# Last 256 tokens of a gated feed-forward layer by seven products: four more waves in a hand-ordered table

## The chip, the cores and the metric

The kernel runs on one core of a Trainium2 chip. The metric is device time in microseconds (us). The core has five engines that each run their own instructions in order and wait for each other through semaphores: TensorE (PE, matmuls; its weight loads are listed as PEld), VectorE (DVE), ScalarE (ACT), GpSimd (POOL) and SyncE (SP), which only starts transfers (DMAs).

## The reference

Polysketch attention (4 batches, 4 heads, 1088 positions, head width 32) gives x, 4352 tokens by 128. A gated feed-forward layer follows, and the change lies in it:

```
gate = 1.0 / (1.0 + np.exp(-(x @ w_gate)))     # x: 4352 x 128, w_gate: 128 x 1536
val = x @ w_val
return (gate * val @ w_out).astype(np.float32)  # w_out: 1536 x 128
```

All is in float32. The 1536 columns are 12 blocks of 128.

## The kernel before

Tokens are worked in chunks of 512 (TCH); HALF is 256. The ninth chunk (number 8) has 256 tokens. Chunks 0 to 4 go through the layer in waves interleaved with the attention of later batches. Chunks 5 to 7 and the last 256 tokens form the *section* (`section`, L1498), in which every instruction of PE, ACT, DVE and POOL is issued in the order of a table, `ORDER` (L19), written out by hand; each engine takes its own items in that order. SP's transfers are issued where the items that call for them stand.

For chunks 5 to 7 gate and value come from Winograd's form of Strassen's scheme: a 2x2 block product by seven products instead of eight. The 2x2 blocks are the two halves of the 128 model features (64 rows of the array each) by two turns of tokens. `load_y` (L443) copies x so that both halves of the features lie in rows 0 to 63 and in rows 64 to 127; `x_sum` (L453, items T) forms four differences of tokens on POOL; `cross_weights` (L463) has made three sums of the weights (fw). One wave covers a pair of the 12 blocks; there are 6 waves for a chunk, 18 in all (w = 0 to 17).

Items of the table, each with a number behind the colon:

- **P1 to P7** (`feature`, L1539): one of the seven products for one block of the wave (the accent marks the second block). An item is two matmuls of 64 rows x 64 columns with 256 tokens. For even waves P1, P2, P3, P5 use the array's low 64 rows (LO) and P4, P6, P7 the high ones (HI); for odd waves the other way round. Two matmuls fill the two column halves of one side, so a LO item and a HI item together fill all four quadrants.
- **Aa, Ac, Sa, Sc** on ACT and **D1, D2, M1, M2** on DVE (`gated`, L1585): Aa copies P1's result to the third bank so that P6, P7, P4 go on from there; Ac copies P5's; D1 and D2 add on DVE; Sa, Sc are sigmoids; M1, M2 multiply gate and value into g. A wave's order is P1, P5; Aa, Ac; P2, P6; D1; P3, P7; D2; P4; Sa, Sc; M1, M2. It uses three PSUM banks, A, C and V, two sets of them in turn (`GA`, `GC`, `V`, L1511).
- **Q0 to Q3** (`token_sum`, L1607): four differences of g on POOL, each 128 x 256. Q0 needs M2, Q1 needs M1 and M2, Q2 needs Q1, Q3 needs Q2.
- **W..** (`w_out`, L1561): the output product, again by seven. WL uses the low rows, WU the high rows (two matmuls of 64 x 64), WF all 128 (two of 128 x 64). The third letter is the bank (A, B), the number the pair of blocks and a part. WxB:p.0 needs Q1 and Q3 of p, WxA:p.0 needs M1 and Q2, WxA:p.1 needs M2 and Q0. Pairs -2 and -1 are the last two of chunk 4, whose sums were formed before the section.
- **EA, EB** (`empty`, L1620) copy the output banks on ACT and start transfers that swap halves (on SP, for chunk 7 on ACT itself: one or two each for EA, three for EB); **F0 to F6** (`total`, L1639) add these up on DVE, transpose, and start four stores on SP.
- For the last 256 tokens (`last`, L1656) the table has plain products: **C0 to C3** are gate and value of a pair of blocks (an item is two matmuls of 128 x 64 with 256 tokens), **Y** the sigmoid, **Z** the product, which also reorders the tokens, and **O0 to O3** the output product (two matmuls of 128 x 64 with 128 columns). `store_end` (L552) copies two banks and stores them from ACT's and SP's queues.

Of the kernel before, what the change touches and what calls it, by code (L numbers as in the profile page):

```python
# [19 lines left out]
WUB:-2.0 P1:0 T0:1 P1':0 P5:1 P1':1 P5:0 P1:1 WLA:-2.1 Aa:0 P5':0 P5':1 Aa:1 P2':0 P6':0 P6:0 P2:0  # L20
Ac:0 P2':1 P6':1 Ac:1 D1:0 P2:1 P6:1 Sa:0 D1:1 P3:0 P7':0 P3':0 P7:0 T2:1 P7':1 P3:1 Sc:0 D2:0 P7:1
P3':1 Sa:1 P1:2 WUB:-1.0 D2:1 P5:2 P4':0 Sc:1 P1':2 P4:0 P4:1 P1:3 M1:0 P1':3 P4':1 P5:3 P5':2 Aa:2
M1:1 WUB:-1.1 WLA:-1.0 Ac:2 P6':2 WLA:-2.0 M2:1 P2:2 P6:2 Aa:3 P2':2 P5':3 Q0:1 D1:2 P6':3 P2':3
Ac:3 P6:3 P2:3 M2:0 Q1:1 P7':2 P3':2 Sa:3 P7:2 WLA:-1.1 D1:3 Q0:0 Sa:2 P3:2 P1:5 D2:2 P7:3 P3:3 Q2:1
Sc:2 P3':3 P7':3 P5:4 P4:2 T1:1 Sc:3 D2:3 P4':2 P1:4 Q3:1 P1':4 WUA:-2.0 M1:2 P5:5 P5':4 Q1:0 P1':5
P4':3 M2:2 Aa:4 WUA:-2.1 P4:3 Ac:4 Q2:0 P2:4 P6':4 M1:3 WLB:-2.0 P6:4 Q3:0 P2':4 WUA:-1.0 Aa:5 D1:4
WLB:-1.1 WUA:-1.1 P6:5 P5':5 M2:3 EA:-1 P7:4 P6':5 Sa:4 P3:4 P7':4 Q0:3 P3':4 P2:5 Ac:5 D2:4
WLB:-1.0 WUA:1.0 Q0:2 Sc:4 P1:6 P2':5 D1:5 P4':4 P1':6 EB:-1 T3:1 P4:4 P7':5 Sa:5 P3':5 P7:5 Q1:2
M1:4 WUA:1.1 P5':6 Q1:3 P1':7 P5:6 D2:5 Aa:6 P3:5 WLB:1.1 Ac:6 M2:4 P6':6 P2:6 Q2:3 P4:5 P6:6 Sc:5
P4':5 WUA:0.1 Q0:4 D1:6 WUA:0.0 WLB:1.0 Q3:3 P1:7 WLB:0.0 M1:5 P7:6 P3':6 M2:5 Q2:2 Aa:7 P7':6 P3:6  # L30
P2':6 P5:7 Sc:6 Q1:4 D2:6 P6:7 P5':7 P2':7 P6':7 F0:-1 Ac:7 T0:2 WLA:3.0 P2:7 WLA:0.0 P4':6 D1:7
Q3:2 Sa:7 P5':8 P4:6 M2:6 Sa:6 P5:8 WUB:1.1 Q2:4 P3':7 P7':7 M1:6 P3:7 P7:7 Q3:4 P1':8 P1':9 Sc:7
D2:7 P1:9 P1:8 Q0:5 Ac:8 WLA:0.1 WUB:0.0 P5:9 P4':7 Aa:8 M2:7 Q0:6 P4:7 WUB:3.0 WLA:3.1 WUB:1.0 Q1:5
M1:7 WLA:1.0 P6':8 WLA:2.1 P6:8 F1:-1 T2:2 Aa:9 P5':9 WLA:2.0 D1:8 WUB:2.0 WLA:1.1 Ac:9 WUB:3.1 P6:9
Q0:7 P7:8 P6':9 P7':8 P3:8 D1:9 Q1:7 P3':8 P2:9 P2':8 P2':9 D2:8 Q2:5 Sc:8 P3:9 P2:8 P3':9 P7:9 M2:8
Q1:6 Sa:8 P4':8 P7':9 Sc:9 P4:8 WLB:3.0 Q3:5 D2:9 WUA:2.0 WLB:2.0 Sa:9 WUA:2.1 WLB:3.1 M1:8 WUA:4.0
P4:9 Q0:8 M2:9 P4':9 P1:11 WUA:4.1 P1:10 Q1:8 M1:9 P1':10 P1':11 P5:11 P5':10 F2:-1 Q2:7 Aa:10 P5:10
WUA:3.0 F3:-1 Aa:11 WUA:3.1 WLB:5.0 Q3:7 F4:-1 P6:10 P2:10 Ac:10 P6':10 WLB:5.1 Q2:6 P6:11 P5':11
D1:10 WUA:5.0 WLB:4.0 Q0:9 Ac:11 WUA:5.1 P6':11 F5:-1 P7':10 P3':10 T1:2 D1:11 P7:10 P3:10 P2':11
P2':10 Q1:9 Sc:10 D2:10 P2:11 P7:11 Sa:10 P7':11 P3:11 T3:2 M2:10 P4:10 WLA:5.1 Sa:11 Q3:6 P4':10  # L40
WLA:5.0 D2:11 P3':11 WLA:4.0 Q2:8 WLA:4.1 WUB:4.0 M1:10 Sc:11 P4':11 WUB:5.1 EA:0 P4:11 WUB:5.0
M2:11 P1':13 P1:12 EB:0 P1:13 P1':12 M1:11 Q0:11 P5:13 P5:12 Aa:12 P5':13 P5':12 F6:-1 Q0:10 Aa:13
WUB:7.0 WLA:7.0 P6:12 WLA:6.0 Ac:12 Q1:10 P6':12 P6':13 Ac:13 WUB:7.1 P2:12 D1:12 Q2:10 P6:13
WUB:6.0 P2':13 WLA:7.1 F0:0 Q1:11 P7':12 P3:12 D1:13 P7:12 P3':12 Q3:10 WLA:6.1 P2:13 Sc:12 D2:12
P3':13 P2':12 Q2:11 P3:13 P7':13 M2:12 Sa:12 P7:13 P4:12 Q3:11 Sc:13 WLB:6.0 P4':12 D2:13 P1:14
WUA:6.0 Sa:13 Q3:8 WLB:7.1 WUA:6.1 M1:12 P4:13 P5':15 Q2:9 M2:13 P4':13 P1:15 WUA:7.0 P1':14 Q3:9
M1:13 WUA:7.1 WLB:7.0 Aa:14 P5:14 P1':15 Q0:12 F1:0 P5:15 P5':14 Aa:15 F2:0 P6:14 P2':14 Q0:13 Ac:14
P6':14 WLB:10.0 WLB:11.0 WUA:9.1 Q1:12 Ac:15 D1:14 WUA:8.1 P6':15 WUA:10.1 P6:15 F3:0 Q2:12 P7':14
P3':14 D1:15 P7:14 P3:14 P2:14 WUA:9.0 Sc:14 D2:14 WUA:10.0 WLB:11.1 Sa:14 WLB:9.1 WUA:11.0 M2:14
WLB:8.0 P4':14 WLB:9.0 P4:14 F4:0 P7:15 WUA:11.1 M1:14 P7':15 P3:15 WUA:8.0 P1':16 D2:15 P1:16  # L50
P3':15 P5':16 P2':15 F5:0 Sc:15 P5:16 P2:15 Aa:16 P4':15 WUB:9.1 P5':17 WLA:8.1 Sa:15 WUB:8.0
WLA:8.0 Ac:16 WLA:10.1 P6:16 M2:15 Q0:14 P6':16 P4:15 WLA:9.1 WUB:9.0 Q1:13 D1:16 P1':17 P2:16
WLA:9.0 P1:17 M1:15 Q3:12 P3:16 P7':16 Aa:17 P3':16 P7:16 Q0:15 WLA:10.0 P5:17 Sc:16 D2:16 WUB:10.0
WLA:11.1 Q2:13 Ac:17 WLA:11.0 P2':17 M2:16 P6':17 P2:17 Q3:13 EA:1 P4:16 P6:17 WUB:11.0 P2':16 Q1:15
D1:17 P4':16 WLA:12.0 Sa:16 Q1:14 WUB:11.1 WLA:13.0 Sa:17 P3':17 P7:17 M1:16 Q0:16 P7':17 P3:17 C1:1
Sc:17 D2:17 Q1:16 C0:1 C3:1 M2:17 Y:1 Q2:16 C2:1 EB:1 C0:0 Z:1 Q0:17 P4:17 WUA:13.0 WLB:13.1
WUA:12.0 Q2:14 F6:0 WLB:12.0 WUA:12.1 WLB:13.0 WUA:13.1 Q3:16 F0:1 C1:0 Q3:14 C2:0 F1:1 Y:0 C3:0
F2:1 Q2:15 C0:3 Z:0 C1:2 Q3:15 WUB:13.1 P4':17 WLA:13.1 WUB:12.0 M1:17 WUB:13.0 WLA:12.1 F3:1 C1:3
# [9 lines left out]
def kernel(  # L68
# [367 lines left out]
    def halves(w):  # L436
        return (HI, LO) if w % 2 else (LO, HI)
# [5 lines left out]
    def load_y(c):  # L443
        t = sbA.tile([P, 2 * H * W1], F32, tag="qp", name="yt")
        y = t[:, : 2 * TCH].rearrange("p (k t) -> p k t", k=2)
        s = t[:, 2 * TCH : 4 * TCH].rearrange("p (u t) -> p u t", u=4)
        YT[c] = y, s
        t0 = tok_chk[SECT + c][0]
        for k, src in enumerate((LO, HI)):
            for dst in (LO, HI):  # L450
                nc.sync.dma_start(out=y[dst, k], in_=xT[src, t0 : t0 + TCH])

    def x_sum(c, u):  # L453
        y, s = YT[c]
# [97 lines left out]
    def store_end(acc):  # L552
# [4 lines left out]
        for u, eng in enumerate((nc.scalar, nc.sync)):  # L557
            eng.dma_start(
                out=bass.AP(
                    tensor=out.tensor,  # L560
                    offset=out.offset + (b * S + r // 32 + u) * DM,
                    ap=[[T * DM, 32], [2 * DM, 4], [1, DM]],
                ),
                in_=o_sb[u],
            )
# [932 lines left out]
    def section():  # L1498
# [22 lines left out]
        sgs = [x[:, : 2 * TCH // 32].rearrange("p (j t) s -> p j (t s)", j=2) for x in sgs]  # L1521
# [11 lines left out]
        def g_of(p):  # L1533
            return held[p][0] if p < 0 else gs[p % len(gs)]
# [4 lines left out]
        def feature(k, nn, w):  # L1539
            lead, tail = halves(w)  # L1540
            j = 2 * (w % per) + nn
            f, gate, val = fw[0][:, :, j], w_sb[:, 0, j], w_sb[:, 1, j]
            y, s = YT[w // per]
            even = w % 2 == 0
            rows, lhsT, rhs, dst = {
                "P1": (lead, gate if even else f[:, 0], y[:, 0, :HALF], GA),
                "P2": (lead, f[:, 0] if even else gate, y[:, 1, :HALF], GA),
                "P5": (lead, f[:, 1], s[:, 0], GC),
                "P3": (lead, f[:, 2], y[:, 1, HALF:], GC),
                "P6": (tail, f[:, 1], s[:, 1], V),  # L1550
                "P7": (tail, f[:, 2 if even else 0], s[:, 2], V),
                "P4": (tail, val if even else f[:, 2], s[:, 3], V),
            }[k]
            start = k in ("P1", "P5") and (k, w) not in started
            for c in range(2):
# [200 lines left out]
```

## Time and profile before

| what | us |
|---|---|
| median of three runs | 283.95 (283.89 to 284.19) |
| span of the profiled execution | 282.5 |
| median less span (what lies around the span) | 1.45 |
| PE busy | 276.7 |
| start of the section's first matmul, from the timeline | 177.27 |
| end of the last matmul | 278.99 |
| the 24 C items (96 records) of PE, busy | 11.5 |
| Y (6 of ACT), busy; Z (6 of DVE), busy | 3.6; 6.7 |
| POOL in the section (72 Q, 8 T, 4 sums of the last held pair) | 65.7 of 101.75 |

The profile's page gives busy time of each engine, 40 slices of the span, the chain of work that ended last, and groups of instructions by line. "L530 PE MATMUL b<-yt,fw 64*64 64x256 f32" is a matmul of line 530 that reads tile yt and weights fw, on 64 rows and 64 columns of the array, with 256 columns streamed. Every float32 matmul leaves two such records. A record lasts longer than the spacing to the next one on its quadrant, since its end includes the drain; spacing is read from start to start. The timeline lists start, length, engine, line, operation and count, and in brackets how long the engine had idled and for whom.

### The profile page before, as it was taken

The page shows a single profiled execution, that of the slowest core. Times are in us where ns is not written, and L with a number is a line of the kernel's source. Part 1 is how long each engine was busy: PE and PEld are TensorE (multiplying, and loading weights), DVE is VectorE, ACT ScalarE, POOL GpSimd, SP SyncE. Part 2 cuts the span into 40 slices and gives each one's busy share as a digit, 9 for nine tenths or more (in the row PEclk, how much of TensorE's full clock was granted, in tenths as well). Part 3 has the DMA queues.
Part 4 walks back from the last instruction along what each step waited for, and adds up shares of the span by engine and source line. Part 5 has one row for each costly group of instructions (what it writes and reads, how often), then busy time and mean ns, then how long its engine had stood idle before and what let it go on. Part 6 is the DMA issues. An engine that isn't in the chain of part 4 may idle for free.

```text
span 282.5 us, 7859 instructions
## 1 busy us (share of the span) xinstructions
PE 276.7 (98%) x3204; PEld 158.6 (56%) x3204; DVE 208.3 (74%) x339; ACT 119.6 (42%) x232; POOL 179.7 (64%) x234
## 2 busy tenths in 40 slices
PE   8899999999999999999999999999999999999994
PEld 3554433354444444544444444577788888875674
DVE  6986789847687777786768857577788968579462
ACT  3689742322326222443225223666554554452130
POOL 2666674567575668664778765547798988197300
PEclk9999999999999999999999999999999999999999
DMA  7995540674681267376348520200310031003133
GB/s 210 334 372 144 119 157 15 167 155 138 198 182 43 41 179 151 95 151 182 74 130 155 134 45 15 64 0 18 89 25 2 2 71 19 2 21 66 24 64 57
DMA packets 33332, 29.02 MB, mean 103 GB/s; under 512 B 19216, under 2 KB 27728, under 8 KB 33296
## 3 DMA queue, kind: packets, MB, share of 16 engines
q1 hardware_dynamic: 28880, 25.44, 37.0%
q10 hardware_dynamic: 4416, 3.08, 4.2%
q8 instruction: 25, 0.41, 0.6%
q14 instruction: 11, 0.09, 0.1%
HBM read 20.60 MB, written 3.26 MB: 84 GB/s over the span
## 4 chain that ended last, share of the span: by engine, by line
PE 97%; ACT 1%; POOL 0%; DVE 0%; issue 0%
PE wave L682 37%; PE b L530 24%; PE prod L530 23%; PE moeout L574 4%; PE warm L379 2%; PE kvz L1027 1%; PE nps L1385 1%; PE kps L808 1%; PE moeout L530 1%; PE kvz L1014 1%; PE cqps L954 1%; PE nps L1217 0%; PE denj L1156 0%; PE nps L1169 0%; PE dps L1198 0%; ACT asb L925 0%
## 5 line engine op out<-in xcount | busy, mean ns | idle before, releaser
L682 PE MATMUL wave<-xT,w_sb 128*64 128x512 f32 (+2 forms) x436 | 117.5, 589 | 0.1
L530 PE MATMUL prod<-tsum,ws 64*64 64x256 f32 (+1 forms) x348 | 81.1, 379 | 0.0
L690 ACT ACTIVATE sg<-wave 128x512 f32<-128x512 f32 x60 | 35.8, 597 | 89.3 <-PE wave L682 85.2
L520 POOL TENSOR_TENSOR tsum<-g,tsum 128x256 f32<-128x256 f32 x48 | 47.2, 982 | 30.5 <-DVE g L717 30.2
L682 PEld LDWEIGHTS wave<-xT,w_sb 128*64 128x64 f32 (+1 forms) x436 | 40.0, 143 | 46.2 <-issue 35.9
L530 PE MATMUL b<-yt,fw 64*64 64x256 f32 x792 | 63.5, 378 | 0.0
L717 DVE TENSOR_TENSOR g<-wave,sg 128x512 f32<-128x512 f32 x60 | 41.1, 685 | 27.2 <-ACT sg L690 26.4
L530 PE MATMUL prod<-g,w_sb 64*64 64x256 f32 (+2 forms) x234 | 53.7, 377 | 0.0
L520 POOL TENSOR_TENSOR tsum<-g 128x256 f32<-128x256 f32 x48 | 40.4, 842 | 16.8 <-DVE g L717 16.5
L530 PEld LDWEIGHTS prod<-tsum,ws 64*64 64x64 f32 (+1 forms) x348 | 42.2, 135 | 11.0 <-issue 6.8
L530 PEld LDWEIGHTS b<-yt,fw 64*64 64x64 f32 x792 | 41.6, 133 | 9.6 <-DVE b L622 0.7
L1618 POOL TENSOR_TENSOR tsum<-g 128x256 f32<-128x256 f32 x36 | 28.8, 815 | 18.4 <-DVE g L1605 8.9
L530 PE MATMUL prod<-g,ws 64*64 64x256 f32 (+1 forms) x116 | 33.5, 377 | 0.0
L530 PEld LDWEIGHTS prod<-g,w_sb 64*64 64x64 f32 (+1 forms) x234 | 25.7, 135 | 13.6 <-issue 9.8
L530 PE MATMUL prod<-tsum,w_sb 64*64 64x256 f32 (+1 forms) x116 | 33.1, 379 | 0.0
L1618 POOL TENSOR_TENSOR tsum<-g,tsum 128x256 f32<-128x256 f32 x36 | 29.1, 819 | 1.1
L530 PE MATMUL b<-yt,w_sb 64*64 64x256 f32 x216 | 25.7, 377 | 0.0
L622 DVE TENSOR_TENSOR b<-b,s 128x512 f32<-128x512 f32 x18 | 12.5, 696 | 8.2 <-PE b L530 7.6
L1605 DVE TENSOR_TENSOR g<-c,sg 128x512 f32<-128x512 f32 x18 | 15.9, 886 | 3.5 <-PE prod L530 2.6
L530 PEld LDWEIGHTS prod<-g,ws 64*64 64x64 f32 (+1 forms) x116 | 15.6, 135 | 3.9
L530 PEld LDWEIGHTS b<-yt,w_sb 64*64 64x64 f32 x216 | 15.5, 133 | 2.4
L1597 ACT ACTIVATE sg<-b 128x512 f32<-128x512 f32 x18 | 10.8, 598 | 14.4 <-PE b L530 14.0
(162 smaller groups left out, 380.4 us busy)
## 6 DMA issues: line engine op xcount, KB each, us to landing
qp<-dq SPq DMA_DIRECT2D x7, 576.0 KB, 5.3
bq<-dq SPq DMA_DIRECT2D x14, 288.0 KB
kq<-in_k_dram SPq DMA_DIRECT2D x3, 544.0 KB
kq<-in_q_dram SPq DMA_DIRECT2D x3, 544.0 KB
w_in<-in_moe_w_out_dram SPq DMA_DIRECT2D x6, 256.0 KB
yt<-xT SPq DMA_DIRECT2D x12, 128.0 KB
w_in<-in_moe_w_gate_dram SPq DMA_DIRECT2D x5, 256.0 KB, 6.7
w_in<-in_moe_w_val_dram SPq DMA_DIRECT2D x5, 256.0 KB, 4.7
```

The lines of the kernel that those rows point to most:

```text
L379: nc.tensor.matmul(out=t[:, 0, :n], lhsT=x, rhs=r, start=True, stop=True)
L520: nc.gpsimd.tensor_tensor(out=t[:, u], in0=in0, in1=in1, op=ALU.subtract)
L530: nc.tensor.matmul(out=out, lhsT=lhsT, rhs=rhs, start=start, stop=stop, skip_group_check=True)
L574: nc.tensor.matmul(out=moe["acc"][d], lhsT=w_sb[:, 2, j, d], rhs=g[:, jj], start=(j == 0), stop=(j == NJ - 1),)
L622: nc.vector.tensor_tensor(out=out, in0=in0, in1=in1, op=ALU.add)
L682: nc.tensor.matmul(out=wv[d, which, jj * tw + o : jj * tw + o + tp], lhsT=w_sb[:, which, j0 + jj, d], rhs=xT[:, t0 + o : t0 + o + tp], sta ...
L690: nc.scalar.activation(out=sg, in_=wv[:, 0], func=ACTF.Sigmoid)
L717: nc.vector.tensor_tensor(out=g, in0=wv[:, 1], in1=sg, op=MUL)
L808: nc.tensor.matmul(out=ts[pi][32 * g : 32 * g + 32, : NJK * 32], lhsT=sk[rows, :], rhs=kT_of[b][rows, KBASE[g] : KBASE[g] + NJK], start=Tr ...
L1597: nc.scalar.activation(out=sg[:, :, second], in_=two(gc), func=ACTF.Sigmoid)
L1605: nc.vector.tensor_tensor(out=g[:, :, second], in0=two(c2), in1=sg[:, :, second], op=MUL)
L1618: nc.gpsimd.tensor_tensor(out=t[:, out], in0=in0, in1=in1, op=ALU.subtract)
```

## The change

The last 256 tokens become four more waves, 18 to 21, of the same scheme. `ends` gives the pairs of blocks of each: wave 18 pairs 0 and 2, wave 19 pairs 1 and 3, wave 20 pair 4, wave 21 pair 5. A P item of these waves is four matmuls of 64 x 64 with 128 tokens (waves 18 and 19 have 14 such items, 20 and 21 seven each). Their Aa to M2 have 512 columns in waves 18 and 19 and 256 in 20 and 21. C, Y and Z go; the 24 O items stay. `load_y` is called for chunk 8 too (four more transfers of half the size), and four T items of 128 columns are added. The whole table is in a new order, and banks and buffers ("homes") are no longer taken in turn by the wave's number but named in the table behind an equals sign (P1:18=1 puts wave 18's bank A in bank 1). `store_end` walks the stored rows in another order.

```
     def load_y(c):
...
+        t0, tw = tok_chk[SECT + c]
+        y = t[:, : 2 * tw].rearrange("p (k t) -> p k t", k=2)
+        s = t[:, 2 * tw : 4 * tw].rearrange("p (u t) -> p u t", u=4)
...
-                nc.sync.dma_start(out=y[dst, k], in_=xT[src, t0 : t0 + TCH])
+                nc.sync.dma_start(out=y[dst, k], in_=xT[src, t0 : t0 + tw])
+
+    def by_turn(x):
+        return x.rearrange("p (y u s) -> p u y s", y=4, u=2)
...
     def store_end(acc):
...
-                    ap=[[T * DM, 32], [2 * DM, 4], [1, DM]],
+                    ap=[[2 * DM, 4], [T * DM, 32], [1, DM]],
...
+        ends = ((0, 2), (1, 3), (4,), (5,))
+
+        def parts_of(w):
+            return len(ends[w - N]) * TCH // 2 if w >= N else TCH
...
         def feature(k, nn, w):
+            if w >= N:
+                for e in range(2):
+                    feature_of(k, w, 2 * ends[w - N][nn] + e, 2 * nn + e, HALF // 2)
+            else:
+                feature_of(k, w, 2 * (w % per) + nn, nn, HALF)
...
             for c in range(2):
                 product(
-                    dst[w % 2][half_of(c), nn * HALF : (nn + 1) * HALF],
+                    bank[home[dst, w]][half_of(c), at * n : (at + 1) * n],
                     lhsT[rows, half_of(c)], rhs[rows], start, False,
                 )
...
         def gated(k, w):
...
+            n = parts_of(w)
+            at = lambda x: bank[home[x, w]][:, :n]
+            s5, c2 = (lambda: s5s[home["s5", w]][:, :n]), (lambda: smalls[home["c2", w]][:, :n])
...
-        def last(k, u, m):
+        def last(u, m):
+            if "end" not in acc:
+                acc["end"] = [bank[x][:, :DM] for x in home["end"]]
...
-                if k[:2] == "P4" and n % per == per - 1 and ("P4", n) in started and n // per + 2 < chunks:
+                if k[:2] == "P4" and n < N and n % per == per - 1 and ("P4", n) in started and n // per + 2 <= chunks:
                     load_y(n // per + 2)
```

The places of the new table that the prediction speaks of:

```
+P5:1=4 P1':0=5 P1:0 P1:1=0 P5':0=1 P1':1 Aa:0=2 WLA:-2.1 WUB:-2.0 Aa:1=3 P5':1 P5:0 P2':0 P6':0 Ac:1=0
+P6':1 P6:0 Ac:0=1 WUB:-1.0 WLA:-1.0 D1:0 P2:1 P6:1 P2':1 P2:0 D1:1 P7':0 P3':0 Sa:0=0 P7:0 P3:0 Sa:1=1
...
+P1':4=0 D2:3=0 P4:2 P1:4 WUA:-1.1 P5:4 Aa:4=3 M1:2 P4':3 P1:5 Ac:4=1 M2:3=3 P4:3 WUA:-1.0 Aa:5=4 WUA:-2.1
+P2':4 M1:3 Q0:3 P6:4 P2:4 P6':4 P6:5 Q0:2 Sa:4=4 P5':5=2 WLB:-1.0 D1:4 Q2:0 P6':5 P5:5 P2:5 WLB:-1.1
+Ac:5=0 Q1:3 P7:4 P3:4 EA:-1 D1:5 P7':4 P3':4 Q1:2 P1:6=0 P2':5 Sc:4=5 D2:4=1 Q2:2 P1':6 WUA:1.1 Sa:5=2
+P3:5 P7:5 T2:1 Aa:6=5 P3':5 P7':5 EB:-1 Q3:2 P5:6=1 WUA:1.0 D2:5=8 P5':6 P4':4 T3:1 P6':6 WLB:1.1 Ac:6=1
+Q3:1 P2:6 P4:4 Sc:5=7 P4:5 P6:6 Q3:0 WUA:0.1 P4':5 D1:6 P2':6 WUA:0.0 Q2:3 M1:4=4 WLB:3.1 P1:7=2 Sa:6=0
+Q3:3 WLB:0.0 P1':7 M2:5=5 WUA:2.0 WLB:1.0 Aa:7=3 P5':7=0 WLB:3.0 M2:4 P6':7 P5:7 P3':6 P7:6 M1:5 Ac:7=0
...
+Sc:10=1 P3':11 WLA:5.1 Sa:11=2 Q3:7 M2:10=3 P4':11 P4':10 Sc:11=5 WLA:4.1 WUB:5.0 Aa:12=1 P4:11 P1':13=3
+EB:0 P5':12=5 P1:13 Q0:10 M1:11=4 EA:0 P5:12 P6:12 T2:2 M1:10 P2:12 P6':12 Aa:13=2 WLA:6.1 WUB:7.0 M2:11
...
+P3:20 M2:17 Ac:21=0 P6:21 WUA:13.0 F5:1 WFA:14.0 Q0:17 F6:1 WFA:14.1 D1:21 Q1:17 WFA:15.1 M1:19=6
+WFB:16.0 Q2:17 M2:19 WFA:15.0 Q3:17 WFA:16.1 WFA:17.0 D2:20=5 WFA:17.1 WFA:16.0 WFB:17.0 EA:2 WFB:17.1
+WFB:15.0 WFB:15.1 WFB:14.0 Sc:20=2 P7:21 EB:2 M2:20=5 P3:21 P4:20 D2:21=8 P2:21 M1:20 P4:21 F0:2 O3:4=2,3
+F1:2 O0:1 Sc:21=1 O2:4 F2:2 Sa:21=4 O0:2 O1:0 F3:2 O0:0 O1:4 M2:21=1 O3:2 M1:21 O3:0 O2:3 O3:3 F5:2 O1:3
+O1:1 F4:2 O0:4 O3:1 F6:2 O0:5 O1:5 O2:1 O2:5 O1:2 O2:0 O3:5 O0:3 O2:2
```

More of the change, by code (lines that the diff above doesn't have):

```diff
@@ L25 @@
[L25 to L30, printed above, removed]
@@ L36 @@
[L36 to L40, printed above, removed]
@@ L41 @@
[L41 to L58, printed above, removed]
@@ new lines @@
+F5:-1 P5:9 WLA:2.1 Q1:6 WLA:1.1 P2':9 Ac:9=0 P7':8 P2':8 D1:9 Q2:6 P3:8 P7:8 Sa:8=1 WLA:4.0 P2:9 D2:8=5
+T1:2 P7:9 WUB:1.0 F6:-1 P3:9 P3':8 Q1:5 P1':10=4 P3':9 Sc:8=2 Q2:5 P7':9 P4':8 Sa:9=3 P4:8 P1:10 Q3:5
+D2:9=6 Sc:9=0 P5:10=1 WUB:4.0 Aa:10=0 M2:7 P5':10 WUB:5.1 P1:11=3 P4':9 Ac:10=1 M1:8=2 Q0:7 P2':10 P1':11
+M2:8 P4:9 P6':10 Aa:11=2 Q1:7 P2:10 WUA:3.0 M1:9=1 P6:10 P6':11 Sa:10=4 WUA:3.1 WLB:5.1 D1:10 Q3:6
+P5':11=5 P6:11 M2:9 WLB:5.0 P5:11 Q2:7 P1':12=4 WUA:5.1 Ac:11=0 P3:10 WUA:5.0 D1:11 P1:12 P7:10 Q0:9
@@ new lines, in last @@
+        def last(u, m):
+            if "end" not in acc:
+                acc["end"] = [bank[x][:, :DM] for x in home["end"]]
+            v, jj = divmod(u, 2)
+            w, nn = [(w, x.index(m)) for w, x in enumerate(ends) if m in x][0]
+            g = end_g(N + w)[:, 2 * nn + jj, v]
+            start = ("end", v) not in started
+            started.add(("end", v))
+            for c in range(2):
+                product(
+                    acc["end"][v][half_of(c)], g[:, half_of(c)], w_sb[:, 2, 2 * m + jj, :], start, False
+                )
@@ L1691, in section @@
         for item in ORDER.split():
+            item, _, at = item.partition("=")
+            at = [int(x) for x in at.split(",") if x]
             k, a = item.split(":")
@@ L1710, in section @@
                 total(int(k[1]), n)
-            elif k[0] in "CYZO":
-                last(k[0], int(k[1]) if len(k) > 1 else 0, n)
+            elif k[0] == "O":
+                last(int(k[1]), n)
             else:
```

166 lines of the change are left out of this document (78 added, 88 removed).

## The prediction

> **What bounds it.** The page first: busy shares, slices, chain.
>
> ```profile
> PE 276.7 (98%) x3204; PEld 158.6 (56%) x3204; DVE 208.3 (74%) x339; ACT 119.6 (42%) x232; POOL 179.7 (64%) x234
> ...
> PE   8899999999999999999999999999999999999994
> ...
> PE 97%; ACT 1%; POOL 0%; DVE 0%; issue 0%
> ```
>
> TensorE is busy in every slice but the last, and the chain that ended last is 97% TensorE. The granted clock is 1.00. The change lies in the section alone, which starts at 177.27 (its first matmul in the timeline), so I took its windows:
>
> ```profile
> 177.25:279.00 101.75, 101.73 (x1705) 78.68 (x1704) 73.92 (x108) 47.51 (x87) 65.70 (x84) 1.00 0.16 32
> ```
>
> Columns: length, then busy us (count) of PE, PEld, DVE, ACT, POOL. Only PE is full. So the section lasts as long as its matmuls take, plus what PE waits. Prices from the timeline (start, length, count):
>
> ```profile
> 202.40 1.94 PE L530 MATMUL b<-yt,fw 64*64 64x256 f32 x32
> 204.13 0.41 PE L530 MATMUL b<-yt,w_sb 64*64 64x256 f32 x2
> ...
> 273.79 0.83 PE L530 MATMUL moeout<-w_sb,g 128*64 128x128 f32 x12
> ...
> 274.45 0.61 PE L530 MATMUL b<-w_sb,g 128*64 128x128 f32 x8
> ```
>
> A product leaves two records. 32 records of 64 rows take 204.13 - 202.40 = 1.73: two table items (one on the low rows, LO; one on the high, HI; eight records) every 0.4327. A C item (128 rows) takes 0.4327 alone. Twelve O records of 128 columns take 0.66, so four (an item) 0.219: half the columns, half the time. Before: 364 P and W items as 182 pairs 78.75, 14 WF 6.06, 24 C 10.39, 24 O 5.25: 100.45. From 177.27 to the last matmul's end (278.99) it is 101.72. The rest is known:
>
> ```profile
> 252.47 1.07 PE L530 MATMUL b<-yt,fw 64*64 64x256 f32 x16
> 253.48 2.38 PE L530 MATMUL b<-xT,w_sb 128*64 128x256 f32 x20
> 255.79 0.43 PE L530 MATMUL b<-yt,fw 64*64 64x256 f32 x2
> ...
> 256.27 0.39 PE L530 MATMUL prod<-g,w_sb 64*64 64x256 f32 x3
> ```
>
> From 252.47 to 256.27 is 3.80, the work in it 2 x 0.4327 + 5 x 0.4327 + 0.4327 = 3.46. Going from 64-row items to 128-row items and back costs 0.33. Before goes in three times and out twice (0.8 in all); 0.17 is the last matmul's tail, 0.3 are short waits in the first 16 us.
>
> **The sum of the matmuls.** Out: 24 C, 10.39. In: 42 P items of waves 18 to 21, each four products of 128 columns. A 64x64 product of 128 columns is in no row; by its neighbours' halving an item takes 0.219 of a pair's time, 9.19 in all. If the shorter stream gained nothing it would be 18.2; below 9.08 (exact halves) nothing can come. I take 9.19, since the 128-column row lies at its half. One in-and-out of the 128-row form goes: -0.33. But the sides no longer match: ahead of the WF block stand 201 LO and 200 HI items, behind it 2 and 3, so each time one side idles for half a pair: +0.44. Together -1.20 - 0.33 + 0.44 = **-1.09**.
>
> That needs the two sides to run independently, for in the new table one side is often an item ahead and two items of one side follow each other. The old table has "P4':5 WUA:0.1" in this order, and:
>
> ```profile
> 201.11 0.38 PE L530 MATMUL prod<-g,ws 64*64 64x256 f32 x1
> 201.14 0.38 PE L530 MATMUL prod<-tsum,ws 64*64 64x256 f32 x1
> 201.15 0.38 PE L530 MATMUL b<-yt,fw 64*64 64x256 f32 x2
> ```
>
> WUA:0.1 (the g,ws and tsum,ws products) starts ahead of P4':5 (yt,fw), which stands before it. Two products are passed here; more isn't shown. Placing the new items one by one, each when its quadrants are free, gives 99.7 if any number may be passed, 101.2 if two, 102.5 if none. The Trainium skill (TensorE: Matmul & The Clock Gate, Part 3, The mechanism) states that matmuls start and end strictly in program order; by that the sum would be the 102.5. The row above speaks against it.
>
> **The waits added,** times from the section's start, an item's place being the items of its side ahead of it times 0.4327.
> *WUB:-1.0* moves from behind P1:2 to place 7: 3.03, at 180.35. It reads the last token sum of the last held pair:
>
> ```profile
> 180.22 0.73 POOL L520 TENSOR_TENSOR tsum<-g,tsum 128x256 f32<-128x256 f32 x1
> ```
>
> That ends at 180.95; with handoff and weight load (0.06 + 0.13) PE resumes at about 181.1. PE is in order ahead of its queue, so everything behind stands: +0.74, and the 0.3 of early waits of before fall into it: +0.44.
> *WLB:3.0*, place 59: 25.53. It needs Q3:3, the 13th of Pool's sums from Q0:3 on, and Q0:3 needs M2:3, behind M1:2, behind P4:2 (33rd HI item, ends 14.28). 14.28 + 0.22 + 0.61 + 0.68 + 0.08 = 15.9. Pool steps 0.69 when alone (two in 1.42 at 187.05): 24.9. But M2 and Pool hold each other up:
>
> ```profile
> 205.56 2.68 POOL L1618 TENSOR_TENSOR tsum<-g,tsum 128x256 f32<-128x256 f32 x3
> ...
> 205.70 1.13 DVE L1605 TENSOR_TENSOR g<-c,sg 128x512 f32<-128x512 f32 x1
> ```
>
> Three sums in 2.68 instead of 2.11, and an M2 of 1.13 instead of 0.68. M2:5 and M2:4 fall in this stretch: 25.8 against 25.4. I take +0.3; ends 0 and, at the 0.83 a sum of 204.87 to 215.70, 1.3.
> *EA:0*: Sc:10 starts at 47.4, then Sa:11, Sc:11, Aa:12, EB:0, EA:0 at 0.55 each end at 50.7; WLA:6.1 reuses the bank at 50.63: +0.2 (0 to 0.5).
> *Other sums*: Q3:11, Q3:10 and Q2:17 end 0 to 0.3 ahead of WLB:11.0, WLB:10.0, WFA:17.0: +0.2 (0 to 0.9).
> *Short chains*: Aa:18 has 0.43 between the end of P1':18 and P6:18, and D1 of waves 13, 17, 20 has 0.87, where Aa needs 0.22 + 0.57 + 0.1 and D1 1.0; P1:21 takes the bank of wave 20's gate 0.44 behind P2:20, where Sa:20 needs 0.7. All but D1:13 and D1:17 fall on the high side while the low one is an item (0.43) ahead, which hides most: +0.25 (0 to 0.8).
> *Wave 21*: P7:21, D2:21, P4:21 follow with nothing between but HI items; 0.22 + 0.42 (256 columns, estimated as half of 0.69 and some) + 0.1, less the 0.44 that this side idles anyway: +0.3 (0 to 0.6).
> None of these can be below 0.
>
> **The rest.** ACT gets 16 instructions for 6 sigmoids (8 of 0.60, 8 of 256 columns, 0.38 between the rows of 512 and 128) and DVE 16 for 6 (about 9.0 for 6.7): +4.2 on 47.5 and +2.3 on 73.9 of 101.7, nothing outside the chains above. Chunk 8's yt is four more DMAs on SP, 2.45 at most (the four of 175.01), queued behind P4:11; EB:0's copies wait behind them, but F0:0 comes 9 us later. If that cover went, F6:0 would be late, which nobody on PE waits for. Four more subtractions on Pool, 1.5 to 2.9, lie 8 us ahead of WFA:17.0. The swapped store moves the same rows.
> **The end:**
>
> ```profile
> 276.47 0.71 DVE L1653 STREAM_TRANSPOSE o_sb<-y 128x512 f32<-128x512 f32 x1
> 277.21 1.95 SPq L542 DMA_DIRECT2D out_dram<-o_sb  x4
> 279.27 0.64 SPq L558 DMA_DIRECT2D out_dram<-o_end  x1
> 279.33 0.64 ACTq L558 DMA_DIRECT2D out_dram<-o_end  x1
> ```
>
> SP's last store follows four of chunk 7, which follow F6:2, 1.8 ahead of PE's end. EB:2 now stands later: its copy, three issues (1.8 on ACT) and a landing (2.1) put F6:2 1.6 to 1.0 ahead of PE's end: +0.15 (0 to 0.75).
>
> **Sum.** -1.09 + 0.44 + 0.3 + 0.2 + 0.2 + 0.25 + 0.3 + 0.15 = **+0.75**. The profiled span of 282.5 becomes 283.2; the median of the runs lies 1.45 above the span, so 283.95 becomes 284.7. A measurement of this kernel can tell 0.2%, 0.57 us, from no change.
>
> **Rivals.**
> *The sums come in time* (0.33): M2 gives way rather than Pool, and the banks are free. Then -1.09 + 0.44 + 0.1 to 0.3: 283.3 to 283.7, half of it faster by 0.2%. For it: before shows hardly a wait of PE on Pool (0.3 us in the section). Against: the sum of before that was due soonest, Q2:17, was done at 263.2, 2 us ahead of WFA:17.0, and in the new table Q3:3 has 0.5 even if nothing holds Pool up. It decides at WLB:3.0: Q3:3 done by 25.4.
> *Pool becomes the bound* (0.15): each sum at 0.89 (205.56) puts Q3:3 at 27.5, 2.0 late, and the later bursts 0.5 late: 283.95 - 1.09 + 0.44 + 2.0 + 0.5 + 0.9 = 286.7. For it the Pool row above; against, the 0.72 a step of 195.88 to 200.18.
> *PE starts products in order* (0.07): +2.8 on the forecast, 287.5.
> My forecast has 0.45, from 283.9 to 285.9, three tenths of it within 0.57. Faster: 0.17; same: 0.16 + 0.14 = 0.30; slower: 0.31 + 0.22 = 0.53. The range leaves out the last rival, the top of the second and little else: 282.9 to 286.6.
>
> **What shows it.** PE's gaps: one of 0.7 near 180.4 on Pool L520; one near 203.5 on a tsum; b<-yt records of 128 columns at 27 ns each with four side by side; 64-row to 128-row changes only around the WF block. Wrong if PE is full until the end (283.2), if the 128-column records stand further apart than 27 ns, or if HI records never pass LO ones.

## The result, and the profile after

The kernel after takes 286.57 us (median of 22 runs) where the kernel before takes 284.18 (22 runs beside them): ratio 1.0086, 95% interval 1.0069 to 1.0103. It is slower by 2.4 us. The forecast was 284.7, +0.75: the direction was right and the size was a third of what came. (The ratios leave out disturbed runs, such as one of the kernel after at a granted clock of 0.754 that took 364.97 us.)

The page of the kernel after (span 284.5 us), TensorE's slices and the chain:

```profile
PE   8899999999999999999999999999999999999993
...
PE 97%; ACT 1%; POOL 0%; DVE 0%; issue 0%
```

Nothing here looks different: TensorE is full to the last slice and is 97% of the chain. The last digit alone hints at something: 3 where it was 4, so the part of the last slice in which TensorE has nothing left is longer.

The section's window, columns as in the prediction (length, then busy us and count of PE, PEld, DVE, ACT, POOL):

```profile
177.00:279.85 102.85, 102.79 (x1945) 89.27 (x1944) 71.97 (x117) 51.32 (x98) 63.34 (x88) 1.00 0.17 35
```

Where it starts shows in the timeline of TensorE:

```profile
176.51 0.59 PE L690 MATMUL wave<-xT,w_sb 128*64 128x512 f32 x1
177.03 0.43 PE L538 MATMUL b<-yt,fw 64*64 64x256 f32 x2
```

The first line is the last matmul ahead of the section, the second P5:1, the first item of the table. From 177.03 to the end of the last matmul at 279.84 it is 102.81 us where before took 101.72 (177.27 to 278.99). So TensorE's part is longer by 1.09; forecast +0.60. Both figures repeat: the traces of the runs below in which TensorE has the order of before (b_store_new, b_pad_act, b_pad_pool) give 101.71 or 101.72, and those with the order of after (a_store_old, a_c7, a_mwalk) 102.83 to 102.86.

The rest lies behind TensorE's end. The timeline of the kernel after from the transpose of chunk 7 on (start, length, engine, line, operation):

```profile
277.40 0.71 DVE L1683 STREAM_TRANSPOSE o_sb<-y 128x512 f32<-128x512 f32 x1
278.14 1.95 SPq L550 DMA_DIRECT2D out_dram<-o_sb  x4
...
279.96 1.13 ACTq L566 DMA_DIRECT2D out_dram<-o_end  x1
280.54 0.65 SPq L566 DMA_DIRECT2D out_dram<-o_end  x1
```

ACT's last store takes 1.13 us to issue (0.64 before), and SP's starts 0.70 behind TensorE's end (0.28 before). From TensorE's end to the end of the span it is 4.64 us; before 3.54. That is another +1.10, where the forecast had +0.15. Now the DMA view of that stretch, first of the kernel before (278.98 to 282.53), then of the kernel after (279.84 to 284.48). The first row is the busy share of the 16 DMA engines in 40 equal slices, in tenths, the second what they moved:

```profile
DMA  8559898659999700017968961300000000000000
GB/s 127 81 88 146 134 138 126 91 82 143 138 140 143 97 4 0 0 29 196 300 185 243 306 179 41 92 0 0 0 0 0 0 0 0 0 0 0 0 0 0
...
q10 hardware_dynamic: 144, 0.07, 6.6%
```

```profile
DMA  9669985899931222222222222220000000000000
GB/s 135 92 91 137 138 122 82 127 139 147 187 39 35 44 57 88 84 88 84 88 66 62 88 88 88 84 71 13 0 0 0 0 0 0 0 0 0 0 0 0
...
q10 hardware_dynamic: 132, 0.07, 5.3%
```

The left block in both is the four stores of chunk 7. What follows are the two last stores. Before, they fill most of the engines for six slices, at 179 to 306 GB/s. After, the row stands at 2 for fourteen slices, at 44 to 88 GB/s: a quarter of the engines' time is busy. The last line says the same in packets: queue 10 (ACT's) carries the 128 rows and 16 small end marks before, 128 and 4 after. The semaphore that tells of a store's landing says so too: it is raised 16 times as the data of SP's last store land before (281.09 to 281.28), and after, behind one early step, 4 times (283.26 to 283.37).

A third part is not in the span at all. Each run lists its time and its span; their difference is 1.74 to 1.95 (median 1.83) in the runs of before that stand beside the experiments, and 2.04 to 2.26 (median 2.08) in those of after. The two do not overlap: +0.25. So the 2.4 us are 1.09 from TensorE's part, 1.10 from the end and 0.25 around the span. The two profiled spans differ by less than the first two, 1.95, because this execution of before came to the section 0.24 later than that of after; the three traces with before's order named above, whose work ahead of the section is the same, come to it at 176.88 to 177.08, and the median span of the runs of before is 282.2 to 282.3, not 282.5.

### The profile page after: what moved, and what is told of

Its sections match the earlier page's. It is cut to its first block, busy times and chain, and to the rows that moved or that the text cites. A ratio compares the mean times of both kernels' runs of the same rounds, so it can differ in the third digit from the quotient of the medians.

```text
span 284.5 us, 8360 instructions
## 1 busy us (share of the span) xinstructions
PE 277.5 (98%) x3444; PEld 169.1 (59%) x3444; DVE 207.1 (73%) x349; ACT 123.2 (43%) x242; POOL 177.5 (62%) x238
## 4 chain that ended last, share of the span: by engine, by line
PE 97%; ACT 1%; POOL 0%; DVE 0%; issue 0%
PE wave L690 36%; PE b L538 25%; PE prod L538 23%; PE moeout L582 4%; PE warm L383 2%; PE kvz L1035 1%; PE nps L1393 1%; PE kps L816 1%; PE kvz L1022 1%; PE cqps L962 1%; PE nps L1225 0%; PE denj L1164 0%; PE nps L1177 0%; PE dps L1206 0%; ACT asb L933 0%; POOL gh L850 0%
## 5 line engine op out<-in xcount | busy, mean ns | idle before, releaser
L538 PE MATMUL prod<-tsum,ws 64*64 64x256 f32 (+1 forms) x348 | 85.7, 379 | 0.0
L538 PE MATMUL b<-yt,fw 64*64 64x256 f32 (+1 forms) x1056 | 77.8, 352 | 0.0
L528 POOL TENSOR_TENSOR tsum<-g,tsum 128x256 f32<-128x256 f32 x48 | 46.2, 963 | 30.3 <-DVE g L725 30.0
L538 PEld LDWEIGHTS b<-yt,fw 64*64 64x64 f32 x1056 | 54.1, 133 | 7.3 <-issue 1.5
L538 PE MATMUL prod<-g,w_sb 64*64 64x256 f32 (+2 forms) x234 | 56.6, 377 | 0.0
L528 POOL TENSOR_TENSOR tsum<-g 128x256 f32<-128x256 f32 x48 | 41.6, 866 | 16.8 <-DVE g L725 16.5
L538 PE MATMUL b<-yt,w_sb 64*64 64x256 f32 (+1 forms) x288 | 30.8, 351 | 0.0
L1648 POOL TENSOR_TENSOR tsum<-g,tsum 128x256 f32<-128x256 f32 x36 | 26.9, 760 | 1.2
L1627 ACT ACTIVATE sg<-b 128x512 f32<-128x512 f32 (+1 forms) x34 | 18.9, 580 | 17.0 <-PE b L538 13.8
L630 DVE TENSOR_TENSOR b<-b,s 128x512 f32<-128x512 f32 (+1 forms) x22 | 14.7, 672 | 10.7 <-ACT s L1625 6.7
L538 PEld LDWEIGHTS b<-yt,w_sb 64*64 64x64 f32 x288 | 18.4, 133 | 1.7 <-ACT b L1623 0.2
L1625 ACT COPY s<-b 128x512 f32<-128x512 f32 (+1 forms) x22 | 12.3, 570 | 10.7 <-PE b L538 10.6
```

The source lines that it names most:

```text
L528: nc.gpsimd.tensor_tensor(out=t[:, u], in0=in0, in1=in1, op=ALU.subtract)
L538: nc.tensor.matmul(out=out, lhsT=lhsT, rhs=rhs, start=start, stop=stop, skip_group_check=True)
L630: nc.vector.tensor_tensor(out=out, in0=in0, in1=in1, op=ALU.add)
L1625: nc.scalar.copy(out=s5(), in_=at("C"))
L1627: nc.scalar.activation(out=smalls[home[k, w]][:, :n], in_=at(k[1].upper()), func=ACTF.Sigmoid)
L1648: nc.gpsimd.tensor_tensor(out=t[:, out], in0=in0, in1=in1, op=ALU.subtract)
```

## The experiments

The theory after the comparison: (1) the swapped walk of the two last stores, whose outermost step has 4 rows and no longer 32, puts them on 4 of 16 DMA engines; (2) SP's last store comes late; (3) TensorE loses time at WUB:-1.0 and on the way out of the 128-row block, as the prediction said; (4) the program's length costs something around the span. The rival for the end is that it is late because of chunk 7's stores; for TensorE that passing between the sides is limited.

### The store's walk: a_store_old, b_store_new

```
 store_end of after (b_store_new: the same two lines of before, the other way)
-                    ap=[[2 * DM, 4], [T * DM, 32], [1, DM]],
+                    ap=[[T * DM, 32], [2 * DM, 4], [1, DM]],
```

> The kernel after with the stored rows walked in the order of the kernel before (the rows of the last 256 tokens land in permuted places: its output is not the reference's). Theory: the swapped walk makes the last two transfers slower: ACT's issue of its store falls back from 1.13 us to about 0.65, the landing from 2.85 us behind SP's issue to about 2.3, so the span shrinks by 0.5 to 0.6 us and the time from 286.57 to about 286.0; if the time around the span (2.06 against 1.45 to 1.68) comes from these transfers too, to about 285.5. Rival (the landing is late because the stores of chunk 7 are still under way, or is chance): 286.5 and both figures stay.

Measured: 286.18 us, 1.0101 times before (1.0051 to 1.0151); its six runs scatter from 285.5 to 289.6, so the time alone decides nothing. The profile does: both stores land by 16 semaphore steps again, ACT's issue takes 0.63 us, and from TensorE's end to the span's end it is 4.02 instead of 4.64. The 0.62 is as expected; the time around the span stays at 2.1, so the stores are not its cause.

> The kernel before with the new walk of the two last stores alone (the rows of the last 256 tokens land in permuted places). Theory (the walk whose outermost step has 4 rows is spread over 4 of the 16 DMA engines, the one with 32 over all 16): the stretch from TensorE's end to the span's end grows from 3.54 us to 4.1 to 4.2, the transfers' rate falls from about 270 to about 80 GB/s, and the time rises by 0.5 to 0.7 us. Rival (the walk only costs something together with the new section, whose end comes on other work): no change. Of the time around the span: if the walk were its cause it would rise from 1.8 to 2.05; expected is that it stays at 1.8.

Measured: 285.54 us, 1.0037 times before (1.0013 to 1.0061), median against median +1.37. One line, in a kernel without any of the other edits, costs 1.0 (by the ratio) to 1.4 us. The end is 4.8 us, ACT's issue 1.42, the time around the span 1.81 as before. Its DMA view from TensorE's end on:

```profile
DMA  7598957998100122225222222222000000000000
```

The same 2s, mostly at 85 GB/s, 132 packets on queue 10, and 4 semaphore steps for each store. TensorE's section is 101.72 as before. The price is twice what was expected. Each store has a quarter of the engines, and the busy share stays at a quarter while both are on their way: it is the same four. Their rows go out nearly one store after the other, 256 packets of 512 bytes at 29 to 31 ns on 4 engines, from 280.25 to 282.20 (1.95 us; 1.80 in the kernel after). They are on their way until 3.5 us behind TensorE's end, in the kernel before until 2.2. The Trainium skill ("DMA: Bandwidth & Descriptors", "Why a DMA increments its semaphore by 16 and not by 1") states the rule: a transfer runs on the largest number of engines up to 16 that divides the slowest dimension of both its access patterns. By it 32 gives 16 and 4 gives 4. The 144 and 132 packets agree.

### Who is late at the end: a_o_swap, a_c7

```
 ORDER of after, a_o_swap
-O2:0 O3:5 O0:3 O2:2
+O2:0 O3:5 O2:2 O0:3
 total of after, a_c7 (chunk 7 alone)
-            store(SECT + c, lambda g4: ...)
+            store(SECT + c, lambda g4: ..., engs=(nc.sync, nc.scalar) * 2)
```

> The kernel after with its last two O items exchanged, so that the bank that ACT copies is finished last and the one that DVE copies for SP's queue 0.22 us earlier, as in the kernel before. Theory: 0.36 us of the longer end is the handoff from DVE to SP's queue (0.37 from the copy's end to the issue, against 0.03 on ACT's own queue); SP's issue then comes at about 280.2 instead of 280.54 and ACT's 0.2 later; the time falls by 0.2 to 0.35, to 286.2 to 286.4. Rival (ACT's long issue of 1.13 us then sets the end, or SP waits for its four earlier stores): no change within 0.1.

Measured: 287.09, 1.0105 (1.0089 to 1.0121): 0.5 us slower than the kernel after, against both expectations. The trace is that of its longest run (289.64; the others took 286.97 to 287.31), so only what lies behind TensorE's end is read from it. SP's store starts at 0.71 behind TensorE's end, as before the edit, though DVE's copy is done 0.22 us earlier; so the handoff was not what it waited for. ACT's store starts 0.22 later and is the first in line on the four engines, so all 256 packets go out later: the end is 5.1 us instead of 4.64.

> The kernel after with two of the four stores of chunk 7 issued by ACT, which is idle there, and not by SP. Theory (SP's last store starts 0.70 us behind TensorE's end because SP is still at the four stores of chunk 7): it starts at 0.37 to 0.40, when DVE's copy is done, and the time falls by 0.3 us, to 286.3. Rival (what SP waits for is another thing, since its last store came at 0.70 also where DVE's copy was done 0.2 us earlier): 0.70 stays and so does the time, within 0.1.

```profile
279.90 1.13 ACTq L566 DMA_DIRECT2D out_dram<-o_end  x1
280.15 0.65 SPq L566 DMA_DIRECT2D out_dram<-o_end  x1
```

The timeline shows the first half of the theory right: without two of the four stores SP starts its last one 0.37 behind TensorE's end (279.78) and not 0.70. The time, 286.52 (1.0085, 1.0056 to 1.0114), does not move. The last rows go out until 3.19 us behind TensorE's end, as in the kernel after (3.20), since SP's packets stand behind ACT's on the same four engines. A wait was taken away, and what is late next is the bound: the four engines. The Trainium skill (same page, "Issuing engines are not separate DMA queues") says that issuing from several engines saves only the time of the issue; here it saved 0.33 of issue and nothing of the time.

### TensorE's first wait: a_wub

```
 ORDER of after
-... P6:0 Ac:0=1 WUB:-1.0 WLA:-1.0 D1:0 P2:1 P6:1 P2':1 P2:0 ...
+... P6:0 Ac:0=1 WLA:-1.0 D1:0 P2:1 P6:1 P2':1 WUB:-1.0 P2:0 ...
```

In the kernel after, the timeline shows the token sum and the weight load that waits for it:

```profile
179.98 0.72 POOL L528 TENSOR_TENSOR tsum<-g,tsum 128x256 f32<-128x256 f32 x1
180.16 0.59 PE L538 MATMUL prod<-tsum,ws 64*64 64x256 f32 x2
...
180.75 0.13 PEld L538 LDWEIGHTS prod<-tsum,w_sb 64*64 64x64 f32 x1 [0.46 <-POOL tsum L528]
```

> The kernel after with WUB:-1.0 moved behind P2':1, two high items later (0.87 us), behind the end of the token sum that it waits for. Theory (forecast's 0.44 net): TensorE's gap of about 0.55 us at 180.2 to 181.0 goes or falls under 0.15, and the time falls by 0.4 to 0.55, to 286.0 to 286.2. Rival: the early waits of ACT's and DVE's first copies, which lie within the gap, come up in its place as in the kernel before (0.3 to 0.5 there): the time falls by 0.1 to 0.2 only.

Measured: 285.97, 1.0061 (1.0046 to 1.0076): 0.60 less than the kernel after. The wait is gone; two early waits show (0.26 for a copy of ACT, 0.23 for D1:0), and the other side hides them. The section takes 102.22 instead of 102.81: 0.59 less, as the median. That is the theory's side, a little above its 0.4 to 0.55 and above the forecast's term (0.44 net).

### The sides of the array: a_sides, a_alt

```
 ORDER of after, a_sides
-P6:21 WUA:13.0 F5:1 WFA:14.0 ... D2:21=8 P2:21 M1:20
+P6:21 WUA:13.0 P2:21 F5:1 WFA:14.0 ... D2:21=8 M1:20
 ORDER of after, a_alt
-P2:18 P3':17                   +P3':17 P2:18
-P7':17 P1:19=5                 +P1:19=5 P7':17
-P3:18 P7':18 ... P6:19 WUA:12.0   +P7':18 P3:18 ... WUA:12.0 P6:19
-P3':19 P7:19                   +P7:19 P3':19
-WUB:12.0 WLA:13.1 M2:18 P1:21=1 P4:19 P5:21=4 P4':19
+WLA:13.1 WUB:12.0 M2:18 P4:19 P1:21=1 P4':19 P5:21=4
-WUB:13.0 P3:20                 +P3:20 WUB:13.0
```

> The kernel after with P2:21 moved ahead of the block of 128-row items, so that 201 low and 201 high items stand ahead of it and two and two behind. Theory (forecast's 0.44 for unequal sides): one side idles half a pair at the way in and at the way out; with equal sides 0.2 to 0.4 us of TensorE's time goes, to 286.2 to 286.4; the wait of P4:21 for D2:21 (0.3) stays. Rival: what idles there is the chain P7:21, D2:21, P4:21, which gets no shorter, so that only the way in is gained: 0.1 to 0.2 us. Second rival: the moved item makes its side pass its neighbours less well: no change.

Measured: 287.31, 1.012 (1.0092 to 1.0147): 0.7 slower than the kernel after by the medians, though its runs scatter from 286.78 to 289.21 and the intervals overlap. The trace is clear: the section takes 103.26 instead of 102.81, 0.45 longer. Equal counts made it worse. The weight load of P4:21 in the kernel after, and then in a_sides:

```profile
272.61 0.44 PEld L538 LDWEIGHTS b<-yt,fw 64*64 64x64 f32 x16 [0.39 <-issue]
...
273.31 0.43 DVE L630 TENSOR_TENSOR c<-b,s 128x256 f32<-128x256 f32 x1
...
273.79 0.41 PEld L538 LDWEIGHTS b<-yt,fw 64*64 64x64 f32 x8
```

```profile
273.53 0.42 DVE L630 TENSOR_TENSOR c<-b,s 128x256 f32<-128x256 f32 x1
...
274.01 0.41 PEld L538 LDWEIGHTS b<-yt,fw 64*64 64x64 f32 x8 [0.30 <-DVE c L630]
```

P4:21 waits for D2:21 in both, 0.48 behind its start. In the kernel after the high side has three items to do meanwhile, in a_sides two: the same stretch with one item less in it. And ahead of the block the high side was not short in time in the kernel after, though it was one item short in number: its last product starts at 266.10, that of the low side at 266.15, since the high side had waited 0.3 for Aa:18 at 254.3. In a_sides the low side starts its last product at 265.93 and the moved item keeps the high one until 266.43. (The section of a_sides begins 0.24 earlier, at 176.79, so its times compare with each other and not one by one with those of the kernel after.) So the forecast's 0.44 for unequal sides was no cost of its own; the spare half pairs lie in the cover of other waits.

> The kernel after with six pairs or triples of neighbours exchanged in the table between P2:18 and the block of 128-row items, so that low and high items stand in turn; the order within each side, and so every bank, buffer and chain, is the same. Theory (an item can start ahead of one of the other side that stands before it only by about one product, so a table that lets one side run ahead costs time): of the 0.35 us that TensorE loses in steps of 0.04 to 0.06 between 256 and 266 us, 0.2 to 0.35 go, and the time falls by as much, to 286.2 to 286.4. Rival (what the prediction assumed: a side passes any number of items of the other; the small losses are weight loads and handoffs): no change within 0.1.

Measured: 286.33, 1.0077 (1.0048 to 1.0105), 0.24 less than the kernel after; with four runs and overlapping intervals the time alone doesn't decide. The chain of work of the kernel after and of a_alt (start, length; the lines are 47 lower in a_alt):

```profile
242.53 2.18 PE b L538 x38
...
266.43 6.25 PE prod L538 x56
```

```profile
242.58 2.18 PE b L491 x38
...
266.10 6.25 PE prod L491 x56
```

From the same work at 242.5 to the first 128-row item it is 23.52 us instead of 23.90, 0.38 less, with the same items in the same order on each side. The stretch repeats to 0.01 where TensorE's order is that of the kernel after (23.90 in a_store_old and a_c7, 23.91 in a_mwalk). So the order in which the table mixes the two sides costs time by itself. Counting every record at its share of the spacing (0.0541 us for 64 rows and 256 columns, half of it for 128 columns, twice for 128 rows), TensorE falls behind by 0.77 us between 255 and 267 us in the kernel after and by 0.43 here. That the cause is a limit on how far one side passes the other is likely, but not shown: by the prediction's working a limit of two products would cost 1.5 us (101.2 less 99.7), though over the whole section. In-order starts would cost far more (2.8 us). The Trainium skill's strict program order ("TensorE: Matmul & The Clock Gate", Part 3, The mechanism) does not hold here (the rows from 201.11 to 201.15 that the prediction shows). Its opposite, that the mix of the sides is free, does not hold either; how many products may be passed was not measured.

### Around the span: b_pad_act, b_pad_pool

```
 store_end of before, ahead of the copies
+        for _ in range(17):     # b_pad_pool: range(5), nc.gpsimd.tensor_copy
+            nc.scalar.copy(out=o_sb[0][:32, :8], in_=w_sb[:32, 2, 0, :8])
```

> The kernel before with 17 small copies added on ACT (as many as ACT has more instructions in the kernel after) ahead of its last copy, where it is idle for 5.3 us; nothing else. Theory (the time around the span is longer in the kernel after, 2.1 against 1.8 us, because one engine's program runs into one more block of instructions, which is fetched behind the span's end): the time around the span rises from 1.82 to about 2.1 and the time by 0.25 us, with the span as before. Rival (it is another engine's program, or no matter of the program's length): 1.82 and 284.2 stay.

Measured: 284.08 (0.9993, 0.9974 to 1.0012), 1.75 to 1.92 around the span, median 1.87: nothing.

> The kernel before with 5 small copies added on GpSimd (as many as it has more instructions in the kernel after) behind its last sum, where it is idle to the end; nothing else. Theory as for the copies on ACT, with GpSimd's program as the one that runs into another block: 2.1 us around the span and 284.45 in all. Rival: 1.82 and 284.2 stay.

Measured: 284.36 against 284.03 for before (ratio 1.0001, 0.9982 to 1.0020, too wide to show 0.25 us), the span unchanged (282.3 against 282.2), and 2.04 to 2.18 around it in each of its runs, median 2.07, where before has 1.75 to 1.95. With five small instructions more on an idle GpSimd it is 0.25 us longer around the span. The DMA view behind the span's end, first of b_pad_act (282.5 to 285), then of b_pad_pool (the same), then of the kernel after (284.5 to 287):

```profile
DMA packets 0, 0.00 MB, mean 0 GB/s; under 512 B 0, under 2 KB 0, under 8 KB 0
```

```profile
DMA packets 1, 0.01 MB, mean 3 GB/s; under 512 B 0, under 2 KB 0, under 8 KB 0
...
q14 instruction: 1, 0.01, 0.9%
```

```profile
q14 instruction: 1, 0.01, 0.9%
```

One more block of instructions is fetched after the last recorded instruction, in the kernels with 323 recorded instructions on GpSimd (waits counted; every trace of an edited kernel after has 323 too, with the fetch and 2.0 to 2.2 around the span), and not in those with 318. The kernel after has the same fetch and the same +0.25, so I put its +0.25 down to this block; that the fetch itself is what takes the time is not shown, and taking five instructions off GpSimd in the kernel after was not tried. The Trainium skill ("Runtime: NRT & Kernel Launch", Instruction fetch mechanics) says that instructions come in blocks (of 16 KiB; the one fetched here has 8 KB) by the sequencer's own DMA and that this is mostly hidden; here it comes when no work is left that could hide it.

### The terms together: a_mwalk, a_best, a_final

a_mwalk gives M1 and M2 of waves 18 to 21 the order of tokens that lets the stores walk as before. a_best is a_mwalk with the edits of a_wub and a_c7. a_final adds a_alt's and moves P3':17 ahead of P6:18.

```
 gated of after (w >= N), with store_end's old walk
-                two = lambda x: x.rearrange("p (q t) -> p q t", t=HALF // 2)
-                g = lambda u: end_g(w)[:, : 2 * n // HALF, u]
+                two = lambda x: x.rearrange("p (q y s) -> p q y s", y=4, s=32)
+                g = lambda u: end_g(w)[:, : 2 * n // HALF, u].rearrange("p q (s y) -> p q y s", y=4)
```

> The kernel after with the reordering of the tokens moved from the store to M1 and M2 of waves 18 to 21, so that the stores walk the rows as before. Theory: the two last transfers run on 16 DMA engines again, ACT's issue takes 0.63 us, 0.62 us of the end goes; each of the eight M items takes up to 0.3 us longer on DVE, those of waves 20 and 21 hold up the transpose of chunk 7 by 0.4 to 0.8 us and with it SP's stores: net -0.6 to 0. Rival (DVE's strided writes cost nothing): -0.6, to 286.0.

Measured: 286.06, 1.0054 (1.0030 to 1.0077), 0.5 less than the kernel after. An M item of 256 columns takes 0.64 us instead of 0.42 and one of 512 columns 1.10 instead of 0.68, more than expected, but in the kernel after DVE is idle for 3.4 us ahead of those of wave 20, and the transpose of chunk 7 starts at 277.45 and not 277.40. SP's last store starts at 0.95 behind TensorE's end and not at 0.70, so of the walk's 0.62 an end 0.38 shorter is left (4.26).

> The kernel after with three edits together: WUB:-1.0 two high items later (alone -0.6), the stores' old walk with the tokens reordered by M1 and M2, and two of chunk 7's stores on ACT. If the terms add up: -0.5 for the wait, -0.6 for the walk, -0.3 for SP, +0.1 for DVE: 285.2 to 285.4, still 1 us above the kernel before, for TensorE's unequal and short waits (0.5 to 1) and the time around the span (0.25) stay. Rival (the gains hide each other, since DVE's longer M items push chunk 7's stores behind): 285.6 to 286.

Measured: 285.27, 1.0022 (0.9993 to 1.0052), 1.3 less than the kernel after: the terms add up. Its section takes 102.22, as in a_wub. Its DMA view from TensorE's end on:

```profile
DMA  9987679999999732986894300000000000000000
```

The second block is the two last stores: up to all engines again, at 174 to 281 GB/s, and the end is 3.60 us. Now that the four engines are no longer the bound, a_c7's edit is worth something: of the end's 1.0 us less, 0.62 is the walk and the rest SP's earlier start.

> All edits to the kernel after that shortened or should shorten something, together: WUB:-1.0 later, the stores' old walk with M1 and M2 reordering the tokens, two stores of chunk 7 on ACT (these three gave 285.27), the alternating neighbours, and P3':17 moved ahead of P6:18, which waits 0.26 us for Aa:18. If the last two give 0.25 each: 284.8, which leaves the time around the span (0.3) and the way out of the 128-row block (0.7) above the kernel before. Rival (the moved P3':17 puts D1:18 and P7:18 later, or passing was not what the alternation cures): 285.1 to 285.4.

Measured: 284.73, 1.0028 (1.0009 to 1.0046). The time is the theory's, but the trace does not show its reason. The section takes 102.15 us, only 0.07 less than in a_best (102.22), and the end 3.62 (3.60). By the count used for a_alt, TensorE falls behind between 256 and 269 us by 0.48 instead of 0.67, but by 0.06 more behind the 128-row block; at 254 us it loses as much as a_best, so the moved P3':17 gave nothing there. The 0.5 between the medians lies ahead of the section as far as the traces go: a_best's profiled execution came to it at 177.43, that of a_final at 176.77, and the runs of a_best alone scatter from 284.6 to 285.5 (one took 287.05). So that 284.73 met 284.8 is luck. It is still 0.7 above the kernel before: 0.25 lie around the span, and 0.43 in the section (102.15 against 101.72). No version here beats the kernel before.

## Why the prediction was right and wrong

**The sum of the matmuls held.** The 128-column products of 64 rows and 64 columns follow each other on a quadrant every 109 ns (255.196, 255.305, 255.414 in the timeline), 27 ns each with four side by side: exact halves, as taken from the neighbouring rows. The C items went and the P items came for -1.2 (-1.3 at exact halves).

**The waits on TensorE were 0.5 larger than forecast, and not the same ones.** Forecast +1.69 with 0.44 for sides and -0.33 for the modes, 1.80 in all; TensorE's losses went from 1.27 (101.72 less 100.45 of work) to 3.56 (102.81 less 99.25), +2.29. The places, by the count of records used for a_alt or by the gaps in the timeline:
- WUB:-1.0: 0.44 forecast, 0.59 shown by a_wub. The forecast let the 0.3 of early waits of before fall into this gap; 0.33 shows between 185 and 191 us instead, at two waits for ACT's copies (0.33 and 0.22 long).
- WLB:3.0: 0.3 forecast, 0.04 in the trace at 204 us (a wait for a copy of ACT beside it makes it 0.10). The rival (sums in time) was right at this place.
- EA:0 and the other sums: 0.4 forecast; 0.47 is lost between 205 and 250 us in steps of up to 0.14, the largest at 230.4. What each step waits for was not traced.
- Short chains: 0.25 forecast, 0.30 at 254.3 for Aa:18 and P6:18, on the side named.
- Way in and out of the block, unequal sides and wave 21: 1.07 forecast (0.44, 0.3 and one in-and-out of 0.33); 0.18 at 266.4, 0.75 from 272.6 to 274.2 and 0.17 at the O items. The sum was right; a_sides shows that it wasn't made of separate terms.
- The mix of the sides: 0 forecast, 0.36 of the section shown by a_alt (102.45 against 102.81). The forecast took the first of the three figures that the prediction listed (99.7, 101.2 and 102.5 for any number of products passed, two and none); it was nearest, but not free.

**What failed is the end.** "The swapped store moves the same rows" was priced at nothing, and the end at +0.15 (0 to 0.75). It moves the same rows over a quarter of the engines. The term measured +1.10: 0.62 from the walk by a_store_old, the rest from SP's later start and the two stores' sharing. b_store_new puts the walk alone at +1.0 to +1.4 in the kernel before. The edit was read as an order of addresses and not as a shape; no row of before shows a transfer with 4 outermost steps, and a term that no row shows should have had two ends. With 1.1 in its place the forecast is 285.65. The direction was right for its reason, since TensorE's part alone is +1.09.

**What was not in the sum at all** is the time around the span, +0.25, most likely by the fetch of one block of instructions. The prediction took it for a constant of 1.45, from the median and another execution's span; single runs give 1.83. With this term too, 285.9; the mix of the sides brings it to 286.25. Of the remaining 0.3, 0.23 is the kernel before itself, which took 283.95 in the three runs that the prediction had and 284.18 in the 22 beside the kernel after; the rest isn't resolved.

Of the signs that the prediction named, the gap at 180.4 on L528 (L520 before), the 27 ns and the mode changes around the block alone were there; the gap near 203.5 was not. None of them looked behind TensorE's end. (Two small slips in the working change nothing: 3.03 from 177.27 is 180.30 and not 180.35, and the first rival's terms give 283.4 to 283.6.)

The rivals: GpSimd did not become the bound (63.3 busy of 102.8, less than before's 65.7), and products did not start in program order.

## What to carry to other kernels

The two things that the forecast missed most stand behind the engine that fills 97% of the chain, where its share of busy time shows nothing: look at the DMA row of the last microseconds, and at run time less span, as well as for stalls. When an edit changes the order in which a transfer walks its rows, ask how many steps its outermost dimension has, and give the answer a price. When a stretch is compared between two kernels, begin both at the same piece of work, and read it in a second execution. And when a wait is taken away without a gain (a_c7), ask which resource the waiting work shares with its neighbour.

## What the runs showed of the hardware

- Two stores of 128 rows of 512 bytes each, from SP and ACT, whose outermost dimension is 4 run at 85 to 88 GB/s at most and land by 4 semaphore steps each; with 32 outermost they reach 272 to 306 GB/s and land by 16. ACT's issue takes 1.13 to 1.42 us with 4 and 0.63 to 0.64 with 32, SP's 0.64 to 0.66 with both.
- The order in which a table mixes products of the low and the high 64 rows costs time though the order on each side is the same: 0.38 us of 23.90 here.
- Five instructions more on GpSimd came with 0.25 us more outside the span and one more fetch of 8 KB of instructions behind it; 17 more on ACT came with neither.
- Open: why SP starts its last store 0.45 us behind the end of its fourth store of chunk 7 in the kernel after and 0.11 in the kernel before. It isn't DVE's copy (a_o_swap).
